# A fused attention and feed-forward block with its gradients: key weights in row pieces, five tiles only centred, two turned tiles copied by VectorE

## The chip, the cores and the metric

The kernel runs on one core of a Trainium2 chip. The metric is the device time of one execution in microseconds; lower is better. The core has five engines that run side by side, each with its own queue in order: TensorE (PE; its weight loads are PEld) multiplies matrices, VectorE (DVE) and ScalarE (ACT) work on tiles of 128 partitions, GpSimd (POOL) does small or slow elementwise work, and SyncE (SP) mostly issues transfers. Products land in PSUM; everything else lies in SBUF, 128 partitions wide. Sixteen DMA engines move data.

## The reference

x is 2048 rows of 640 features, bf16. The kernel returns the block's output and six gradients (the vector-Jacobian product with grad_out).

```python
def _A_ref(x, wqkv, wo):
    B, S, D = x.shape
    H = 32; Dh = D // H
    qkv = (x @ wqkv).reshape(B, S, 3, H, Dh).transpose(2, 0, 3, 1, 4)
    q, k, v = qkv[0], qkv[1], qkv[2]
    phi = lambda t: jnp.where(t > 0, t + 1, jnp.exp(t)) + 1e-6
    pq, pk = phi(q), phi(k)
    kv = jnp.einsum("bhsd,bhse->bhde", pk, v)
    z = jnp.einsum("bhsd->bhd", pk)
    num = jnp.einsum("bhqd,bhde->bhqe", pq, kv)
    den = jnp.einsum("bhqd,bhd->bhq", pq, z)[..., None] + 1e-6
    return (num / den).transpose(0, 2, 1, 3).reshape(B, S, D) @ wo
...
h = x + _A_ref(_layernorm(x), A_wqkv, A_wo)
h2 = h + _B_ref(_layernorm(h), B_w1, B_w3, B_w2)   # silu(x@w1) * (x@w3) @ w2
...
_out, _vjp = jax.vjp(_f, A_x, A_wqkv, A_wo, B_w1, B_w3, B_w2)
```

(The first lines are shortened: the reference writes the transposes through small lambdas.)

## The kernel before

The order of the work is written out by hand: each engine executes its instructions in the order in which the Python code emits them, and the framework adds the waits between engines. The rows of x form 16 tiles of 128 rows (ST = 16); the 640 features form 5 chunks of 128 (DT = 5) or two halves of 320 (HD).

The change lies in the first stage, which computes, for each tile t of x: the layernorm, the transposed normalized tile, the key product (tile times the 640 key columns of wqkv), and phi of it, stored in pk_all. Query tiles are interleaved from tile 6 on, at t = 6, 7, 9 and 11 (QT).

**Statistics and norm (class Stats).** Per tile VectorE runs two BatchNormStats over 320 columns each (L148), an aggregate (L151) and an addition of eps (L154, ve); POOL raises it to -0.5 (L155, rs). The norm (L161) subtracts the mean and multiplies by rs on VectorE, in place in x_sb. For even tiles from 10 on ScalarE does the norm instead (norm_act, L166), with a bias that POOL makes. Tile 0 is only centred (RAW = 1): its rs is applied as the scale of ScalarE's Exp and Relu instead, and p1_scale (L264, "C" in the steps) multiplies x by rs later on VectorE, since later work reads the scaled x.

**Turning a tile.** For tiles 0 to 7, p1_tr makes five transposes on TensorE into a PSUM tile (L258) and ScalarE copies them to pqT (L260). Tiles 8 to 15 are turned by a DMA transpose that SP issues after the norm (L251).

**Key product.** p1_mm makes two halves of five matmuls each (L268, 128x320), with the next tile's turning between them ("between"). The accumulators ("big") have two buffers. Tile 0 has its own path (first, kh, act): two separate PSUM tiles and four activations of 320 columns (L535).

**phi.** ScalarE computes Exp into mq and Relu into rq (L295, L296). The rest is held back: VectorE's min-and-add (L299) and the addition into pk_all or, for a query, into its own tile (L300). mq and rq have three buffers each, used in turn by all phis: those of key tiles 0 to 6, query 0, key 7, query 1, key 8 and so on.

**v_steps.** For each t this table lists what VectorE does after the key product was emitted: ("S", t) statistics of a tile, ("N", t) its norm, ("C", t) the scaling, R the oldest rest that is held. "A", "B" and "L" are norms placed behind the phi of that step.

**Beside it.** At t = 3 to 6 a chunk of another product (gp, L395, five matmuls of 512 columns) is computed and copied by ScalarE (L420). From t = 7 on m_part accumulates pk transposed times x (macc, L430) for the tiles in M0.

**Loads.** SP issues, in this order: x tiles 0 and 1, the key weights' first half of columns (load_wq(2, 3): all five row chunks, 320 columns), x tile 2, their second half, x tile 3, x tiles 4 and 5; then transposed loads of w2 and of grad_out, x tiles 6 to 9, the query weights (load_wq(0, 2)), x tiles 10 to 15. The weights w1 and w3 follow at t = 4, 5, 6 and 12 (trickle).

**The start.** TensorE runs 34 products of 128 columns on ones while the first loads come in (warm_up, L468), and 8 more after the turning of tile 0.

**The end.** The last stage makes 128-row jobs of the gradients of w1 and w3 (grad_job); the first seven jobs store their result in two halves each.

Of the kernel before, what the change touches and what calls it, by code (L numbers as in the profile page):

```python
# [9 lines left out]
P = 128  # L10
BF16 = mybir.dt.bfloat16
F32 = mybir.dt.float32
ALU = mybir.AluOpType
AF = mybir.ActivationFunctionType
# [4 lines left out]
S, D, H, F = 2048, 640, 32, 1728  # L19
DH = D // H  # L20
ST, DT = S // P, D // P
# [3 lines left out]
HD = D // 2  # L25
# [30 lines left out]
def kernel(  # L56
# [19 lines left out]
    V, A, T, G, SY = nc.vector, nc.scalar, nc.tensor, nc.gpsimd, nc.sync  # L76
    dma, dmaT, dmaG = SY.dma_start, SY.dma_start_transpose, G.dma_start
# [36 lines left out]
    x_sb = x_ext[:, :, 0:D]  # L114
# [16 lines left out]
    class Stats:  # L131
# [10 lines left out]
                for j in range(2):  # L142
                    self.part(src, t, j)

        def part(self, src, t, j, mid=None):
            if j == 0:
                self.st[t] = cp.tile([P, 2, 6], F32, name="st6", bufs=4)
            V.bn_stats(out=self.st[t][:, j, :], in_=src[:, t, j * HD:(j + 1) * HD])  # L148
            if j == 0:
                return  # L150
            V.bn_aggr(out=self.mv[:, t, :], in_=self.st.pop(t)[:])  # L151
            if mid is not None:
                mid()
            V.tensor_scalar(out=self.ve[:, t:t + 1], in0=self.mv[:, t, 1:2], scalar1=EPS_LN, scalar2=None, op0=ALU.add)  # L154
            G.tensor_tensor(out=self.rs[:, t:t + 1], in0=self.ve[:, t:t + 1], in1=mhalf[:, 0:1], op=ALU.pow)  # L155

        def center(self, out, src, t):
            V.tensor_scalar(out=out, in0=src, scalar1=self.mv[:, t, 0:1], scalar2=None, op0=ALU.subtract)
# [14 lines left out]
    ln1, ln2 = Stats("ln1"), Stats("ln2")  # L173
# [5 lines left out]
    ps = pool("p1p", space=PSUM)  # L179
    wqkv = U1.tile([P, DT, 3 * D], BF16, name="wqkv", tag="D")  # L180
    wq_v = A_wqkv.rearrange("(c p) n -> p c n", p=P)

    def load_wq(a, b):
        dma(out=wqkv[:, :, a * HD:b * HD], in_=wq_v[:, :, a * HD:b * HD])

    def load_x(a, b):
        dma(out=x_sb[:, a:b, :], in_=xS[:, a:b, :])

    load_x(1, 2)
    A.activation(sg[:], zero[:], AF.Exp)  # L190
    load_wq(2, 3)
    load_x(2, 3)
    load_wq(3, 4)
    load_x(3, 4)
    load_x(4, 6)

    mask = cp.tile([P, DT, M_MAX], BF16, name="mask")

# [40 lines left out]

    XT_DMA = 8  # L240
    WARM = 34
    RAW = 1

    def on_act(t):
        return t > XT_DMA and t % 2 == 0
# [1 line left out]
    def p1_norm(t):  # L247
        xn = x_sb[:, t, :]
        (ln1.norm_act if on_act(t) else ln1.norm)(xn, xn, t)
        if t >= XT_DMA:  # L250
            dmaT(out=pqT[:, :, t * P:(t + 1) * P], in_=xn)  # L251

    def p1_tr(t, parts=((0, DT),)):
        xn = x_sb[:, t, :]
        for a, b in parts:
            tr = ps.tile([P, DT, P], BF16, name="tr", bufs=2)
            for c in range(a, b):
                T.transpose(tr[:, c, :], xn[:, c * P:(c + 1) * P], ident[:])  # L258

            A.copy(out=pqT[:, a:b, t * P:(t + 1) * P], in_=tr[:, a:b, :])  # L260

    def p1_scale(t):
        xn = x_sb[:, t, :]
        V.tensor_scalar(out=xn, in0=xn, scalar1=ln1.rs[:, t:t + 1], scalar2=None, op0=ALU.mult)  # L264

    def p1_half(acc, t, n0):
        for c in range(DT):
            T.matmul(acc, lhsT=pqT[:, c, t * P:(t + 1) * P], rhs=wqkv[:, c, n0:n0 + HD], start=(c == 0),  # L268
                     stop=(c == DT - 1))

    def p1_acc():
        return ps.tile([P, 2, 512], F32, name="big", bufs=2)

    def p1_mm(t, n0, between=None, halves=None):
        acc = p1_acc() if halves is None else None
        for j in range(2):
            p1_half(acc[:, j, 0:HD] if halves is None else halves[j][:, 0:HD], t, n0 + j * HD)
            if j == 0 and between is not None:
                between()
        return acc  # L280

    def two(ap):
        return ap.rearrange("p (j n) -> p j n", j=2)
# [3 lines left out]
    def phi_tiles():  # L287
        return [p1.tile([P, D], BF16, name=n, bufs=3) for n in ("mq", "rq")]

    def phi(acc, dst, t, parts=None):  # L290

        mq, rq = parts or phi_tiles()
        if parts is None:
            kw = dict(scale=ln1.rs[:, t:t + 1]) if t < RAW else {}
            A.activation(two(mq[:]), acc[:, :, 0:HD], AF.Exp, **kw)  # L295
            A.activation(two(rq[:]), acc[:, :, 0:HD], AF.Relu, **kw)  # L296

        def rest():
            V.tensor_scalar(out=mq[:], in0=mq[:], scalar1=1.0, scalar2=1e-6, op0=ALU.min, op1=ALU.add)  # L299
            V.tensor_tensor(out=dst, in0=mq[:], in1=rq[:], op=ALU.add)  # L300
        held.append(rest)
# [157 lines left out]
    zero_pads()  # L459
    load_w2T(0, 2 * P)  # L460
    load_g2T(0)
    load_x(6, 10)
    load_w2T(2 * P, 4 * P)
    load_wq(0, 2)
    load_x(10, ST)
    def warm_up(n, warm):
        for _ in range(n):
            T.matmul(warm[:, 0:P], lhsT=ones[:], rhs=ones[:], start=True, stop=True, skip_group_check=True)  # L468
# [12 lines left out]
    def stat(t):  # L481
        ln1.run(x_sb, t, t + 1)
        if on_act(t):
            ln1.bias(t)
# [1 line left out]
    ln1.part(x_sb, 0, 0)  # L486
    ln1.part(x_sb, 0, 1, center_first)
    p1_tr(0, ((0, 2), (2, DT)))
    warm_up(8, p1_acc()[:, 0])
    stat(1)  # L490
    p1_norm(1)
    ln1.part(x_sb, 2, 0)
    ln1.part(x_sb, 2, 1)
    ln1.part(x_sb, 3, 0)
    p1_norm(2)
    ln1.part(x_sb, 3, 1)
    ln1.part(x_sb, 4, 0)
    p1_norm(3)
    ln1.part(x_sb, 4, 1)
    w13 = [go for c0, c1 in ((0, 2), (2, 4), (4, 5)) for go in load_w13(c0, c1)]  # L500
    w13 += [lambda: dma(out=w1[:, :, F:FP], in_=rows(B_w3)[:, :, F - FL:F])]

    def load_wo():
# [2 lines left out]
    trickle = {4: w13[0], 5: lambda: w13[1](0, 1), 6: lambda: w13[1](1, 2), 12: w13[2]}  # L506

    R = None
    v_steps = {1: (R, ("N", 4)), 2: (("S", 5), R, ("N", 5)), 3: (("S", 6), R, ("N", 6), ("C", 0)),
               4: (("S", 7), R, ("N", 7), ("S", 8)), 5: (R, ("N", 8), ("S", 9)), 6: (R, ("N", 9), ("S", 10)),  # L510
               7: (("S", 11), R, R, ("A", 10), ("L", 11)), 8: (("S", 12), R, R, ("S", 13)),
               9: (("N", 13), R, ("S", 14), ("B", 12)), 10: (R, R, ("S", 15)), 11: (R, ("A", 14), ("L", 15))}
    V_OPS = {"S": stat, "N": p1_norm, "C": p1_scale}

    def xn_out(g, q):
        sl = slice(g * TPC, (g + 1) * TPC)
# [9 lines left out]
    M0 = {7: (0, 1, 2), 8: (3, 4, 5)}  # L526
    M0.update({t: (t - 3,) for t in range(9, ST)})
    for t in range(ST):
        first = None
        if t < RAW:  # L530
            first = phi_tiles()
            kh = [ps.tile([P, 512], F32, name="k0", tag="m", bufs=2) for _ in range(2)]

            def act(i, j):
                A.activation(first[i][:, j * HD:(j + 1) * HD], kh[j][:, 0:HD], (AF.Exp, AF.Relu)[i],  # L535
                             scale=ln1.rs[:, t:t + 1])

            def between():
                act(0, 0)
                p1_tr(t + 1)  # L540
                act(1, 0)
            k = p1_mm(t, D, between, kh)
            act(0, 1)
            act(1, 1)
        else:
            k = p1_mm(t, D, (lambda: p1_tr(t + 1)) if t + 1 < XT_DMA else None)
        steps = v_steps.get(t, (R,) * len(held))
        for step in steps:
            if step is R:
                held.pop(0)()  # L550
            elif step[0] in V_OPS:
                V_OPS[step[0]](step[1])
        phi(k, pk_all[:, t, :], t, first)
        for when in ("A", "B", "L"):
            for step in steps:
                if step is not R and step[0] == when:
                    p1_norm(step[1])
            if when == "A" and t in QT:
                q_tile(QT.index(t))
        if 3 <= t < 7:  # L560
            ghh_chunk(t - 3, lambda: ps.tile([P, 512], F32, name="gp", tag="m", bufs=2))
        m_part(0, M0.get(t, ()))
        if t >= 11:
            V.memset(bd[:, t - 11, :], 0.0)
            make_mask(t - 11)
        if t >= 9:
            m_part(1, [2 * (t - 9), 2 * (t - 9) + 1])
        for f, *n in outs.get(t, ()):
            f(*n)
        if t in trickle:  # L570
            trickle[t]()
# [983 lines left out]
    for i, (f0, f1) in enumerate(blocks):  # L1555
        n = f1 - f0
        for m in range(DT):
            last = (i, m) == (len(blocks) - 1, DT - 1)
            for a, b in ((0, n - P), (n - P, n)) if last else ((0, n),):
                c = (a + b) // 2  # L1560
                halves = ((a, c), (c, b)) if i * DT + m < 7 else ((a, b),)
                out = [(x + y - a, z + y - a, to) for y, w in halves for x, z, to in both_grads(m, f0 + y, f0 + w)]
                grad_job(hnN, m, lambda t: gb[i][:, t, a:b], b - a, out, A.dma_start)
        load_block(i + 2)
        if 0 < i <= 4:
            gw2_out(i - 1)
        if i < 4:
            gw2_turn(i)
# [36 lines left out]
```

## Time and profile before

| what | value |
|---|---|
| median of 3 runs | 820.98 us (819.28 to 821.57) |
| the profiled execution | 820.36 us |
| its span | 818.64 us |
| PE busy | 811.6 us (99%) |
| DVE busy | 452.7 us (55%) |
| ACT busy | 324.8 us (40%) |
| POOL busy | 131.7 us (16%) |
| granted TensorE clock | 1.00 |

The span is the time from the first to the last instruction in the profile; the execution's own time has 1.7 us more around it. Times in the profile are counted from the start of the span. An engine's busy time says little by itself: what counts is which engine or transfer the chain of work goes through at a given moment. In lines of the timeline the first number is the start, the second the time of one instruction or of a group of equal ones; overlapping neighbours on one engine start before the previous one's recorded end.

### The profile page before, as it was taken

Reading aid. Unit: us, or ns where it says so; the run is one execution under the profiler, and the core shown is the slowest. Engines: PE = TensorE matmul, PEld = TensorE weight load, DVE = VectorE, ACT = ScalarE, POOL = GpSimd, SP = SyncE. Lnnn points to the kernel's source line nnn. Section 1 sums busy time; section 2 is a strip of 40 time slices with the busy share of each in tenths; the row PEclk is TensorE's granted clock in tenths of the full one; section 3 lists DMA queues with packets and bytes.
Section 4 is the critical chain, followed back from the end, with each engine's and each line's share of the span. In section 5 each row is a group of like instructions: output and inputs, shape, how many; then the busy total and the mean of one; then the engine's idle time right before and its main releaser. Section 6 shows DMA issues by size and latency. Waiting matters only on the chain.

```text
span 818.6 us, 13711 instructions
## 1 busy us (share of the span) xinstructions
PE 811.6 (99%) x5261; PEld 501.6 (61%) x5292; DVE 452.7 (55%) x973; ACT 324.8 (40%) x609; POOL 131.7 (16%) x198
## 2 busy tenths in 40 slices
PE   9999999999999999999999999999999999999998
PEld 6777544555555555754577777777777777544444
DVE  7859997998898566300057777772781544200000
ACT  7856688665565666011112212222212334211111
POOL 2243333323222212100001111110220000000000
PEclk9999999999999999999999999999999999999999
DMA  9899899696485556999877877269994888979991
GB/s 262 207 242 277 206 276 302 207 244 174 128 209 158 169 168 168 239 254 243 233 178 181 218 194 193 58 111 181 269 217 93 179 193 153 249 175 235 221 239 37
DMA packets 335889, 162.46 MB, mean 198 GB/s; under 512 B 252560, under 2 KB 329072, under 8 KB 335824
## 3 DMA queue, kind: packets, MB, share of 16 engines
q1 hardware_dynamic: 291920, 120.68, 63.8%
q0 software_dynamic: 7328, 24.48, 8.9%
q10 hardware_dynamic: 36576, 16.42, 8.2%
q8 instruction: 41, 0.67, 0.3%
q14 instruction: 24, 0.20, 0.1%
HBM read 47.09 MB, written 53.43 MB: 123 GB/s over the span
## 4 chain that ended last, share of the span: by engine, by line
PE 96%; DMA 1%; ACT 1%; DVE 1%; issue 0%; SPq 0%; POOL 0%; DVEq 0%
PE mm L395 20%; PE job L1335 19%; PE ghn L1131 14%; PE gxn L1504 8%; PE gw L1086 7%; PE big L268 4%; PE o L913 4%; PE o L859 3%; PE gwo L1219 3%; PE macc L430 3%; PE gr L1188 3%; PE dkv L1441 3%; PE at L657 2%; DMA wqkv<-in_A_wqkv_dram 1%; PE dkv L1369 1%; DMA tri<-tri 1%
## 5 line engine op out<-in xcount | busy, mean ns | idle before, releaser
L1335 PE MATMUL job<-gb,hnN 128*128 128x496 bf16 (+3 forms) x576 | 116.8, 366 | 0.0
L1131 PEld LDWEIGHTS <-ggb 128*128 128x128 bf16 x864 | 84.5, 98 | 33.0
L395 PE MATMUL mm<-pqT,w 128*128 128x512 bf16 x396 | 93.2, 379 | 0.5
L1335 PEld LDWEIGHTS <-hnN 128*128 128x128 bf16 x576 | 55.8, 98 | 61.0
L395 PEld LDWEIGHTS <-w 128*128 128x128 bf16 x540 | 52.6, 98 | 62.9 <-issue 0.6
L1339 ACT CAST obs<-job 128x496 bf16<-128x496 f32 (+4 forms) x56 | 28.5, 510 | 123.6 <-PE job L1335 123.6
L1131 PE MATMUL ghn<-w13a,ggb 128*128 128x320 bf16 x448 | 63.5, 299 | 0.0
L1146 DVE SCALAR_TENSOR_TENSOR wb<-gs,hnb 128x640 f32<-128x640 bf16 x16 | 13.2, 825 | 88.1 <-ACT gs L1143 88.1
L1131 PE MATMUL ghn<-w13b,ggb 128*128 128x320 bf16 x416 | 61.4, 299 | 0.0
L395 PE MATMUL mm<-g2T,w2T 128*128 128x512 bf16 x228 | 58.8, 379 | 0.6
L1086 PE MATMUL gw<-hb,g 128*128 128x512 bf16 (+2 forms) x316 | 58.4, 345 | 0.2
L1086 PEld LDWEIGHTS <-g 128*128 128x128 bf16 x320 | 31.3, 98 | 27.0
L420 ACT CAST ghh<-mm 128x512 bf16<-128x512 f32 x48 | 28.2, 588 | 48.2 <-PE mm L395 41.4
L1196 POOL TENSOR_TENSOR sz<-Zb,g_h 128x640 f32<-128x640 bf16 x16 | 20.2, 1262 | 163.7 <-DVE g_h L1197 163.7
L796 ACT ACTIVATE sig<-mm 128x512 bf16<-128x512 f32 x56 | 33.7, 602 | 25.0 <-PE mm L395 21.6
L1143 ACT ACTIVATE gs<-ghn 128x640 bf16<-128x640 f32 x16 | 11.3, 705 | 76.0 <-PE ghn L1131 76.0
L395 PEld LDWEIGHTS <-w2T 128*128 128x128 bf16 x260 | 25.4, 98 | 23.4
L268 PEld LDWEIGHTS <-pqT 128*128 128x128 bf16 x320 | 30.7, 98 | 13.5 <-ACT pqT L260 0.9
L268 PE MATMUL big<-wqkv,pqT 128*128 128x320 bf16 x250 | 38.4, 299 | 0.2
L1335 PEld LDWEIGHTS <-g 128*128 128x128 bf16 x320 | 31.0, 98 | 11.5
L832 DVE TENSOR_TENSOR gate<-gate,sig 128x1024 bf16<-128x1024 bf16 x28 | 19.3, 689 | 33.9 <-ACT gate L807 31.1
L1091 ACT CAST gw2o<-gw 128x512 bf16<-128x512 f32 (+2 forms) x20 | 10.4, 519 | 66.6 <-PE gw L1086 25.3
(217 smaller groups left out, 1391.2 us busy)
## 6 DMA issues: line engine op xcount, KB each, us to landing
hh_d<-hhT SPq DMA_DIRECT2D x24, 256.0 KB, 2.8
gg_d<-gate POOLq DMA_DIRECT2D x24, 256.0 KB, 4.4
gg_d<-ghh POOLq DMA_DIRECT2D x24, 256.0 KB, 4.1
ggb<-gg_d SPq DMA_DIRECT2D x6, 896.0 KB, 5.3
ggb<-gg_d ACTq DMA_DIRECT2D x6, 832.0 KB, 5.7
ggb<-gg_d SPq DMA_DIRECT2D x2, 1728.0 KB, 13.9
pk_d<-pk_all SPq DMA_DIRECT2D x4, 640.0 KB, 5.4
g<-in_grad_out_dram SPq DMA_DIRECT2D x4, 640.0 KB, 5.7
```

Of the source, the lines that this page charges most:

```text
L268: T.matmul(acc, lhsT=pqT[:, c, t * P:(t + 1) * P], rhs=wqkv[:, c, n0:n0 + HD], start=(c == 0), stop=(c == DT - 1))
L395: T.matmul(acc[:], lhsT=w[:, c, fc * P:(fc + 1) * P], rhs=rhs[:, c, :], start=(c == 0), stop=(c == DT - 1))
L420: A.copy(out=ghh[n // 2][:, n % 2, :], in_=acc[:])
L430: T.matmul(macc[m][j][:, 0:n], lhsT=pk_all[:, t, m * P:(m + 1) * P], rhs=x_ext[:, t, j * HD:j * HD + n], start=(t == 0), stop=(t == ST - 1))
L796: A.activation(sig[:, i, :], gp[:], AF.Sigmoid)
L859: T.matmul(accs[i, j][:, 0:HD], lhsT=hhT[c][:, fc, i * P:(i + 1) * P], rhs=w2[:, fc, j * HD:(j + 1) * HD], start=(first and fc == 0), stop ...
L913: T.matmul(o2["ps"][:, 0:HD], lhsT=hhT[c][:, fc, i * P:(i + 1) * P], rhs=w2[:, fc, j * HD:(j + 1) * HD], start=(fc == 0), stop=(fc == FT - 1))
L1086: T.matmul(acc[:, 0:fw], lhsT=g2[:, t, m * P:(m + 1) * P], rhs=hb[b][:, t, 0:fw], start=(t == 0), stop=(t == ST - 1))
L1131: T.matmul(acc[:, j, 0:HD], lhsT=ggb[t // 2][:, k, lo:lo + P], rhs=rhs[:, j * HD:(j + 1) * HD], start=(k == 0), stop=(k == NG - 1))
L1335: T.matmul(acc[:, 0:n], lhsT=lhs[:, t, m * P:(m + 1) * P], rhs=rhs(t), start=(t == 0), stop=(t == ST - 1))
L1339: A.copy(out=ob, in_=acc[:, 0:n])
L1504: T.matmul(acc[:, j, 0:HD], lhsT=g, rhs=wqT[:, k, j * HD:(j + 1) * HD], start=(k == 0), stop=(k == 14))
```

## The change

- The key weights come in two row pieces: row chunks 0 and 1 with all 640 columns ahead of x tile 2, chunks 2 to 4 behind it. The x loads are regrouped (4 to 6, then 7 to 9), and the query weights come in two loads.
- Tile 0's product goes chunk by chunk over both halves (first_mm), with the turning of tile 1 behind the first two chunks; its special phi path goes.
- Tiles 0 to 4 are only centred (RAW = 5); their rs goes into Exp and Relu, and POOL instead of VectorE scales x for these five tiles, at t = 3 to 6.
- The turned tiles 2 and 3 are copied by VectorE; the others still by ScalarE.
- From t = 3 on, the turning of the next tile comes behind both halves of the key product instead of between them.
- Statistics, norms and rests stand one step later in v_steps for t up to 7, with the query rests following.
- Four warm-up products instead of eight behind the turning of tile 0.
- In the last stage six instead of seven jobs store in two halves.

```diff
-        def part(self, src, t, j, mid=None):
+        def part(self, src, t, j, mid=None, end=True):
...
-            if j == 0:
-                return
+            if j and end:
+                self.end(t, mid)
+
+        def end(self, t, mid=None):
             V.bn_aggr(out=self.mv[:, t, :], in_=self.st.pop(t)[:])
             if mid is not None:
                 mid()
...
+    def load_wk(a, b):
+        dma(out=wqkv[:, a:b, D:2 * D], in_=wq_v[:, a:b, D:2 * D])
+
     load_x(1, 2)
     A.activation(sg[:], zero[:], AF.Exp)
-    load_wq(2, 3)
+    load_wk(0, 2)
     load_x(2, 3)
-    load_wq(3, 4)
+    load_wk(2, DT)
     load_x(3, 4)
-    load_x(4, 6)
+    load_x(4, 7)
...
-    RAW = 1
+    RAW = 5
...
-    def p1_tr(t, parts=((0, DT),)):
+    def p1_tr(t, parts=((0, DT),), copy=A.copy):
...
-            A.copy(out=pqT[:, a:b, t * P:(t + 1) * P], in_=tr[:, a:b, :])
+            copy(out=pqT[:, a:b, t * P:(t + 1) * P], in_=tr[:, a:b, :])
...
-        V.tensor_scalar(out=xn, in0=xn, scalar1=ln1.rs[:, t:t + 1], scalar2=None, op0=ALU.mult)
+        G.tensor_scalar(out=xn, in0=xn, scalar1=ln1.rs[:, t:t + 1], scalar2=None, op0=ALU.mult)
...
-    def p1_mm(t, n0, between=None, halves=None):
-        acc = p1_acc() if halves is None else None
+    def p1_mm(t, n0, between=None, at=0):
+        acc = p1_acc()
         for j in range(2):
...
-            if j == 0 and between is not None:
+            if j == at and between is not None:
                 between()
         return acc
 
+    def first_mm(between):
+        acc = p1_acc()
+        for c in range(DT):
+            for j in range(2):
+                T.matmul(acc[:, j, 0:HD], lhsT=pqT[:, c, 0:P], rhs=wqkv[:, c, D + j * HD:D + (j + 1) * HD],
+                         start=(c == 0), stop=(c == DT - 1))
+            if c == 1:
+                between()
+        return acc
...
-    load_x(6, 10)
+    load_x(7, 10)
     load_w2T(2 * P, 4 * P)
-    load_wq(0, 2)
+    load_wq(0, 1)
+    load_wq(1, 2)
...
-    warm_up(8, p1_acc()[:, 0])
-    stat(1)
-    p1_norm(1)
-    ln1.part(x_sb, 2, 0)
-    ln1.part(x_sb, 2, 1)
-    ln1.part(x_sb, 3, 0)
-    p1_norm(2)
-    ln1.part(x_sb, 3, 1)
-    ln1.part(x_sb, 4, 0)
-    p1_norm(3)
-    ln1.part(x_sb, 4, 1)
+    warm_up(4, p1_acc()[:, 0])
+    for t in (1, 2):
+        ln1.part(x_sb, t, 0)
+        ln1.part(x_sb, t, 1, lambda: center(t))
+    ln1.part(x_sb, 3, 0)
+    ln1.part(x_sb, 3, 1, end=False)
...
-    v_steps = {1: (R, ("N", 4)), 2: (("S", 5), R, ("N", 5)), 3: (("S", 6), R, ("N", 6), ("C", 0)),
-               4: (("S", 7), R, ("N", 7), ("S", 8)), 5: (R, ("N", 8), ("S", 9)), 6: (R, ("N", 9), ("S", 10)),
-               7: (("S", 11), R, R, ("A", 10), ("L", 11)), 8: (("S", 12), R, R, ("S", 13)),
-               9: (("N", 13), R, ("S", 14), ("B", 12)), 10: (R, R, ("S", 15)), 11: (R, ("A", 14), ("L", 15))}
-    V_OPS = {"S": stat, "N": p1_norm, "C": p1_scale}
+    v_steps = {1: (("E", 3), ("P", 4, 0)), 2: (("P", 4, 1), ("E", 4), R), 3: (("S", 5), R, ("N", 5), ("C", 0)),
+               4: (("S", 6), R, ("N", 6), ("C", 1)), 5: (("S", 7), R, ("N", 7), ("S", 8), ("C", 2), ("C", 3)),
+               6: (R, ("N", 8), ("S", 9), ("C", 4)), 7: (R, R, ("N", 9), ("S", 10), ("S", 11), ("A", 10), ("L", 11)),
+               8: (("S", 12), R, R, ("S", 13)), 9: (("N", 13), R, ("S", 14), ("B", 12)), 10: (R, R, ("S", 15)),
+               11: (R, R, ("A", 14), ("L", 15))}
+    V_OPS = {"S": stat, "N": p1_norm, "C": p1_scale, "E": lambda t: ln1.end(t, lambda: center(t)),
+             "P": lambda t, j: ln1.part(x_sb, t, j, end=False)}
...
+        turn = (lambda: p1_tr(t + 1, copy=V.tensor_copy if t in (1, 2) else A.copy)) if t + 1 < XT_DMA else None
+        k = p1_mm(t, D, turn, int(t > 2)) if t else first_mm(turn)
...
-                halves = ((a, c), (c, b)) if i * DT + m < 7 else ((a, b),)
+                halves = ((a, c), (c, b)) if i * DT + m < 6 else ((a, b),)
```

## The prediction

> **What bounds the kernel now.** I read the page's chain first, then busy time by window, the chain in order of time up to 16 us, the timelines of VectorE and ScalarE from 27 to 33 us, and who ScalarE waits for.
>
> ```profile
> PE 96%; DMA 1%; ACT 1%; DVE 1%; issue 0%; SPq 0%; POOL 0%; DVEq 0%
> 0.00:15.00 15.00, 12.99 (x109) 9.81 (x111) 10.44 (x39) 10.33 (x18) 3.77 (x12) 1.00 0.93 233
> 15.00:42.00 27.00, 26.95 (x197) 18.64 (x197) 24.38 (x77) 23.14 (x37) 6.98 (x14) 1.00 0.86 229
> ```
> The first line is the chain by engine; the others give window, length and then busy us of PE, PEld, DVE, ACT, POOL. TensorE carries the chain, so whatever idles it moves the end. From 15 to 42 us it idles 0.05 us; VectorE is busy 24.38 of 27, so it has little room in just the stage to which the change gives it other work.
>
> ```profile
> 2.77 5.33 DMA wqkv<-in_A_wqkv_dram
> 8.10 0.04 issue
> 8.14 0.84 PE k L268 x5
> ...
> 9.99 0.69 ACT pqT L260
> 10.68 0.69 ACT mq L295
> 11.38 0.59 ACT rq L296
> 11.97 0.67 ACT pqT L260
> 12.63 0.05 issue
> 12.68 0.85 PE big L268 x5
> ```
> The head's chain (start, us): the second half of the key weights lands at 8.10, and from 9.99 to 12.63 ScalarE is what TensorE waits for: two copies of turned tiles with an Exp and a Relu between them. That is what the change attacks.
>
> ```profile
> 28.14 0.32 DVE L299 TENSOR_SCALAR mq<-mq 128x640 bf16<-128x640 bf16 x1
> 28.56 0.49 DVE L300 TENSOR_TENSOR pk_all<-mq,rq 128x640 bf16<-128x640 bf16 x1
> 28.97 0.32 DVE L299 TENSOR_SCALAR mq<-mq 128x640 bf16<-128x640 bf16 x1
> 29.40 0.49 DVE L300 TENSOR_TENSOR hx<-mq,rq 128x640 bf16<-128x640 bf16 x1
> 29.81 0.44 DVE L161 TENSOR_SCALAR x_sb<-x_sb,ln_mv,ln_rs 128x640 bf16<-128x640 bf16 x1
> 30.16 0.88 DVE L148 BATCH_NORM_STATS2 st<-x_sb 128x6 f32<-128x320 bf16 x2
> ```
> VectorE's timeline: the rest of phi (min, add) of key tile 6, of query tile 0 (it writes hx), then the norm of tile 11 and the statistics of tile 12.
>
> ```profile
> ACT mq L295 <- DVE pk_all L300: 2.4, 4, 0.8
> ```
> ScalarE's waits from 24 to 44 us (total, times, longest). mq and rq have three buffers each, so an Exp waits for the rest three phis before it. Key tile 8's Exp is the eleventh phi, query tile 0's the eighth: Exp 8 (30.34 in ScalarE's timeline) needs the rest that ends at 29.89. The ring has almost no slack now.
>
> **How I cost it.** I list each engine's instructions in their new order; each starts when its engine is free and its inputs are there (+0.04 us, the chain's "issue" steps). Start-to-start times come from the timeline: half product 0.68, turning a tile 0.28, gp 1.08, macc 0.82; ScalarE Exp or Relu 0.60 (0.69 with a scale), copy 0.68; VectorE statistics pair 0.92, aggregate 0.24, eps 0.08, min 0.42, add 0.41, norm 0.36; POOL's rs 0.56. The same list for the old order gives norm 9 at 25.32 (trace 25.34), Exp 8 at 30.31 (30.34), the products of tile 9 at 30.64 (30.74): good to about 0.2 us.
>
> **The change, part by part.**
>
> *Row pieces.* Both pieces move the same 800 KB, in packets of 1280 B instead of 640 B. The packet records give 55 and 32 ns, so an engine needs 40 x 55 = 2.20 us instead of 80 x 32 = 2.56. I take the second piece at 8.10 - 0.36 = 7.75 (bounds 7.0, if the long first packets of the slowest engine go away, and 8.1), the first, two rows of five, at 6.2 instead of 6.58. The third x tile that shares a load with tiles 4 and 5 adds 0.44 us there, and tile 4 is first read at 10.9; splitting the query weights adds an issue of 0.58 us on SP and 0.36 us of packets, before a use at 22.
>
> *Only centred, copies on VectorE.* Tile 1 no longer waits for its rs. Scaling moves into Exp and Relu (0.79 against 0.70 us each, on a ScalarE that has lost two copies). VectorE's copy out of PSUM has no row at 128x640; L1422 takes 0.280 us for 256 columns and 0.345 for 384, which continues to 0.48 (bounds 0.35 and ScalarE's 0.69). TensorE then runs: rest of tile 0 at 7.79, tile 1 at 8.61, turn of tile 2 at 9.29 to 9.57, VectorE's copy 9.78 to 10.26, tile 2 at 10.33, copy of tile 3 11.50 to 11.98, tile 3 at 12.02: **0.6 us earlier** than in the list of before (12.64). But the first copy is queued in front of the aggregate and centring of tile 3, so VectorE idles 0.6 us until tile 2 is turned.
>
> *Transposes behind the products.* From tile 4 on, gp (1.08 us) hides ScalarE's copy (0.69). Tile 5's turning wants, at 16.10, a norm that VectorE ends at 16.39: 0.3 us lost. What is left is **0.3 us earlier** from tile 5 to tile 8.
>
> *The rests one step later.* v_steps takes the first rest at tile 2 instead of 1, so at tile 7 the two rests are those of tiles 5 and 6, not 6 and query 0. VectorE starts norm 9 at 26.49 instead of 25.32: 0.83 for the rest of tile 6 that now stands ahead of it, 0.34 for the two copies (0.82) less the scaling that went (0.30) and an earlier start. Then the rest of query 0 comes behind norm 11 (0.36) and the statistics of tile 12 (1.24), and norm 11 follows eps 11 directly, so that VectorE stands 0.75 us waiting for rs 11 (POOL 0.56 and both hops). It ends at 29.90 + 0.34 + 0.36 + 1.24 + 0.75 = **32.59**. Behind it on ScalarE waits Exp 8: 32.63 to Relu's end at 33.93, 2.3 us late; and Exp of query 1 waits behind ScalarE's norm of tile 10 (rs 10 late), until a Relu end of 31.23. TensorE has two accumulators: tile 9 is ready at 30.31 and starts at 31.27 (0.96), query 2 at 32.63 and starts at 33.97 (1.34), query 3 at 39.69 and starts at 40.27 (0.58). 2.88 - 0.33 = **2.55 us later**, by tile 12.
>
> *Scaling on POOL.* Five tensor_scalar of 128x640. Rows around it: a memset of 64x512 0.54 us, a two-input product of 128x640 1.26; I take 0.9. Three (tiles 0, 1, 2) run beside statistics. But tiles 2 and 3 follow each other, and rs 9 and tile 4 stand behind them.
> ```profile
> 59.94 1.86 DVE L299 TENSOR_SCALAR mq<-mq 128x640 bf16<-128x640 bf16 x1
> 60.07 1.54 POOL L367 TENSOR_TENSOR pr<-hx,Zb 128x320 f32<-128x320 bf16 x2
> ```
> Here the min, 0.32 us elsewhere, took 1.86 while POOL multiplied: it waited for both products. With that, the rest of tile 5 waits 0.65 us for tile 3's scaling and the add of tile 6 waits 0.8 for tile 4's: +1.45, so 4.0 us later in all. Bounds: 0 (the form doesn't collide, or VectorE comes first) and +2.75 (at 1.26 us each). The row is the nearest, but who comes first is open; I take +0.9.
> The Trainium skill (GPSIMD Engine Reference, 3.1 Elementwise) puts a GpSimd loop with little work at 1.03 cycles an element, at 1.2 GHz an estimate of 0.55 us for 640; by it the sum would be 3.0 us instead of 4.0. No row here shows the form.
>
> *Hidden.* Tile 8's DMA transpose is issued at 23.7 (before 23.39) behind one more weight load; at 2.6 us to landing, or 3.8 behind that load, it is there by 27.5, wanted at 28.1. POOL's scalings end by 27.5; tiles 0 to 2 are read at 27.3 with their own done at 24.6. Storing the seventh weight-gradient job in one piece lies in 640 to 815 us, where TensorE is busy all 175 us and ScalarE 43.75: nothing. Without that cover, one issue is about half a microsecond.
>
> **Sum.** -0.33 + 2.88 + 0.9 = +3.4 us, of which nothing is won back: after 42 us TensorE idles 5 us in all, in waits behind its own work. The profiled execution took 820.36 us (span 818.64 and 1.7 around it): 823.8. The median of the runs lies 0.62 above it, 824.4. I say **824.1**. Of before, 0.3% is 2.46 us, about what a measurement of this kernel can tell from no change.
>
> **Rivals.**
> *It bites less* (0.22). No collision on POOL, and early weights: 7.0 also moves VectorE's first waits, and the list gives +1.8 to +2.55 for 7.0 to 7.75, 822.2 to 823.4. For it: POOL's small rs never lengthened a neighbour. Against: the two L299 lines.
> *Head gain alone* (0.12). Exp 8 finds its buffer free: this decides at about 30.3 us, when the rest of query 0 must be done. Then 0.3 to 1.1 us are won, 819.9 to 820.7, and with much earlier weights 818.5. For it: ScalarE's stretch 9.99 to 12.63 does go. Against: VectorE would have to be 2.3 us ahead of the list.
> *POOL scaling is dear* (0.06). At 2.0 us each, rs 9 and the rests queue up behind it: list +9, 829. For it: POOL's pace on products, 2 ns an element; against: one input, not two.
> *Late clock* (0.04). Matmuls of 128 columns are 107 ns apart until 6.1 us and 56 from 7.3 on: the faster pace came 5.1 us after the first product (1.13). Four of the eight warm-up products go, which leaves TensorE idle just before 6.2. If it had to start afresh there, all up to 11.3 would run at half pace; the 3.5 us from 7.79 on would do 1.75 us of work: 825.8. Against: the gap is 0.3 us. The Trainium skill (TensorE: Matmul & The Clock Gate, Part 1) has the pace set by free-running windows of 3.4 us; by it the delay would end at 9.6, an estimate of 0.9 us. No run here shows either.
>
> **Numbers.** Forecast 0.56 (own range 823.4 to 826). Slower by over 0.3%: 0.56 + 0.06 + 0.04 = 0.66. Within: 0.22 and 0.08 of the head gain, 0.30. Faster: the remaining 0.04. The range leaves out the better half of the head gain and dear scaling: 820.4 to 826.8.
>
> **What would show it.** Right: tile 3's products near 12.0; a VectorE wait for rs 11; min of query 0 after 31.5; an Exp of ScalarE waiting over 1 us for VectorE's add; TensorE idle some 3 us between 30 and 41. POOL's scaling: its duration, and a min or add above 0.5 us beside it. Wrong: TensorE without gaps there, or gaps before 28 us (then norms 5 to 7 are later than listed).

## The result and the profile after

The changed kernel takes 826.01 us (median of 5 runs, 825.74 to 826.90). The kernel before, run beside it, takes 820.44 us (819.26 to 821.57). The ratio is 1.0074, 95% interval 1.0062 to 1.0085: 0.74% slower. The profiled execution took 826.61 us, its span is 824.5 us, against 818.64 before: 5.86 us more.

Line numbers from here on are those of the changed kernel unless said otherwise: L148 statistics, L153 aggregate, L156 eps, L157 rs on POOL, L160 centring, L163 norm, L168 the norm that ScalarE does, L265 the copy of a turned tile, L269 the scaling on POOL, L273 and L291 the products, L309 and L310 Exp and Relu, L313 and L314 min and add of a rest, L444 the gradient products (macc).

The page's chain of work by engine:

```profile
PE 93%; DVE 3%; DMA 2%; ACT 1%; issue 0%; SPq 0%; POOL 0%; DVEq 0%; ACTq 0%
```

Busy time by window (length, then PE, PEld, DVE, ACT, POOL, the granted clock, DMA share and GB/s):

```profile
0.00:15.00 15.00, 12.73 (x106) 9.95 (x108) 10.04 (x37) 8.69 (x14) 3.48 (x11) 1.00 0.91 228
15.00:42.00 27.00, 22.62 (x160) 14.82 (x160) 23.83 (x68) 18.98 (x31) 16.39 (x18) 1.00 0.74 200
```

VectorE's share of the chain went from 1% to 3%. From 15 to 42 us TensorE is busy 22.62 us where it was 26.95, and POOL 16.39 instead of 6.98. VectorE works nearly as long as before in this window (23.83 against 24.38), but gets less far.

The chain in order of time in the head (start, us):

```profile
2.71 5.47 DMA wqkv<-in_A_wqkv_dram
8.19 0.04 issue
8.23 0.98 PE big L291 x6
9.20 0.68 PE big L273 x5
9.88 0.28 PE tr L263 x5
10.16 1.51 PE big L273 x10
11.67 0.29 PE tr L263 x5
11.96 0.02 issue
11.99 0.49 DVE pqT L265
12.48 0.41 DVE st L148
```

The second piece of the key weights is there at 8.19, not earlier than before (8.10). ScalarE's copies have left the head of the chain, as meant, but at 11.99 VectorE enters it and carries it up to 39.6 us, apart from 17.4 to 24.2, where it runs through TensorE and one copy on ScalarE, and two rs on POOL. What that does to TensorE is in its timeline; the last brackets are idle time and who ended it:

```profile
29.44 1.52 PE L273 MATMUL big<-wqkv,pqT 128*128 128x320 bf16 x10
30.80 0.98 PE L444 MATMUL macc<-x_sb,pk_all 128*128 128x320 bf16 x6
34.54 1.52 PE L273 MATMUL big<-wqkv,pqT 128*128 128x320 bf16 x10 [2.76 <-ACT rq L310]
37.00 1.52 PE L273 MATMUL big<-wqkv,pqT 128*128 128x320 bf16 x10 [0.94 <-ACT rq L310]
```

These are tile 8, the gradient products, tile 9 and query 2. With 0.33 us at query 3 the stalls are 4.03 us. Tile 12 starts at 45.37 where it started at 39.98 (the first line is of the kernel before): **5.4 us of the 5.86 are lost by then**.

```profile
39.98 1.52 PE L268 MATMUL big<-wqkv,pqT 128*128 128x320 bf16 x10
45.37 1.52 PE L273 MATMUL big<-wqkv,pqT 128*128 128x320 bf16 x10
```

ScalarE's waits from 24 to 44 us (total, times, longest) say whom it waited for:

```profile
ACT x_sb L168 <- POOL nb L172: 2.8, 1, 2.8
ACT mq L309 <- DVE hx L314: 2.7, 2, 1.5
```

The 2.8 us are the norm of tile 10, which ScalarE does itself: it stands in front of query 1's Exp and waits for a bias that POOL can only make after VectorE's statistics of tile 10. The 2.7 us are Exp 8 (1.16) and query 2's Exp (1.54), which wait for adds. VectorE's own timeline shows why all of it is late:

```profile
24.62 0.92 DVE L163 TENSOR_SCALAR x_sb<-x_sb,ln_mv,ln_rs 128x640 bf16<-128x640 bf16 x1
...
26.68 0.72 DVE L313 TENSOR_SCALAR mq<-mq 128x640 bf16<-128x640 bf16 x1
27.51 0.49 DVE L314 TENSOR_TENSOR pk_all<-mq,rq 128x640 bf16<-128x640 bf16 x1
27.92 0.58 DVE L313 TENSOR_SCALAR mq<-mq 128x640 bf16<-128x640 bf16 x1
28.60 0.49 DVE L314 TENSOR_TENSOR pk_all<-mq,rq 128x640 bf16<-128x640 bf16 x1
29.01 0.92 DVE L163 TENSOR_SCALAR x_sb<-x_sb,ln_mv,ln_rs 128x640 bf16<-128x640 bf16 x1
```

Norm 9 begins at 29.01. In the kernel before it was this line:

```profile
25.34 0.44 DVE L161 TENSOR_SCALAR x_sb<-x_sb,ln_mv,ln_rs 128x640 bf16<-128x640 bf16 x1
```

Norms that took 0.44 us take 0.92, mins that took 0.32 take 0.72 and 0.58, while the adds are 0.49 as ever. Beside them POOL scales:

```profile
16.30 1.96 POOL L269 TENSOR_SCALAR x_sb<-x_sb,ln_rs 128x640 bf16<-128x640 bf16 x1
...
24.50 3.81 POOL L269 TENSOR_SCALAR x_sb<-x_sb,ln_rs 128x640 bf16<-128x640 bf16 x2
28.29 0.62 POOL L157 TENSOR_TENSOR ln_rs<-ln_ve,mhalf 128x1 f32<-128x1 f32 x1
28.91 1.94 POOL L269 TENSOR_SCALAR x_sb<-x_sb,ln_rs 128x640 bf16<-128x640 bf16 x1
```

One scaling takes 1.9 us. Against their times in the kernel before, four norms are longer by 0.48 and two mins by 0.40 and 0.26: 2.58 us that VectorE loses.

### The profile page after: what moved, and what is told of

Its sections match the earlier page's. It is cut to its first block, busy times and chain, and to the rows that moved or that the text cites. A ratio compares the mean times of both kernels' runs of the same rounds, so it can differ in the third digit from the quotient of the medians.

```text
span 824.5 us, 13717 instructions
## 1 busy us (share of the span) xinstructions
PE 812.3 (99%) x5257; PEld 501.1 (61%) x5288; DVE 455.7 (55%) x974; ACT 323.8 (39%) x605; POOL 141.0 (17%) x203
## 4 chain that ended last, share of the span: by engine, by line
PE 93%; DVE 3%; DMA 2%; ACT 1%; issue 0%; SPq 0%; POOL 0%; DVEq 0%; ACTq 0%
PE mm L409 20%; PE job L1331 19%; PE ghn L1127 14%; PE gxn L1500 8%; PE gw L1082 7%; PE o L909 4%; PE o L855 3%; PE gwo L1215 3%; PE gr L1184 3%; PE dkv L1437 3%; PE big L273 2%; PE macc L444 2%; PE at L653 2%; DVE st L148 1%; DMA wqkv<-in_A_wqkv_dram 1%; PE mm L273 1%
## 5 line engine op out<-in xcount | busy, mean ns | idle before, releaser
L273 PE MATMUL big<-wqkv,pqT 128*128 128x320 bf16 x250 | 38.1, 299 | 4.0 <-ACT rq L310 4.0
L273 PEld LDWEIGHTS <-pqT 128*128 128x128 bf16 x310 | 29.9, 98 | 17.0 <-issue 3.9
## 6 DMA issues: line engine op xcount, KB each, us to landing
ggb<-gg_d ACTq DMA_DIRECT2D x6, 832.0 KB, 5.7
```

## The experiments

All are read by two numbers: the median of the runs, and the start of tile 12's products in the one profiled execution, which shows what the first 45 us cost without the scatter of what follows. It does contain the scatter of the first loads: VectorE's first copy of a turned tile waits for them, and in the profiles that have this copy it starts between 9.10 and 10.20 us (10.20 in the change). "Later" is against 39.98 in the kernel before. The median of the kernel before was 820.44 beside the changed kernel, 820.28 beside the first four runs, 820.05 beside the next four, 819.88 beside the last four.

| kernel | median us (range, runs) | ratio to before (95%) | tile 12 at | later |
|---|---|---|---|---|
| the change | 826.01 (825.74–826.90, 5) | 1.0074 (1.0062–1.0085) | 45.37 | 5.39 |
| no_scale | 824.22 (823.17–826.01, 5) | 1.0050 (1.0038–1.0062) | 42.71 | 2.73 |
| scale_vec | 825.46 (824.25–827.43, 5) | 1.0069 (1.0056–1.0082) | 44.17 | 4.19 |
| rest_early | 826.87 (824.03–828.76, 6) | 1.0076 (1.0060–1.0092) | 44.71 | 4.73 |
| copy_act | 825.17 (823.57–825.94, 5) | 1.0062 (1.0049–1.0075) | 43.86 | 3.88 |
| cols | 827.00 (825.40–827.57, 4) | 1.0081 (1.0066–1.0096) | 44.90 | 4.92 |
| rows_only | 822.60 (821.03–824.71, 9) | 1.0028 (1.0014–1.0042) | 40.42 | 0.44 |
| norm10_behind | 825.75 (825.29–828.40, 5) | 1.0076 (1.0059–1.0093) | 45.69 | 5.71 |
| keep_busy | 829.92 (829.24–832.01, 4) | 1.0124 (1.0108–1.0140) | 44.96 | 4.98 |
| turn_mid | 825.25 (824.90–827.46, 5) | 1.0069 (1.0056–1.0081) | 44.92 | 4.94 |
| light2 | 822.33 (821.78–824.38, 5) | 1.0036 (1.0022–1.0049) | 41.04 | 1.06 |
| light3 | 822.18 (821.95–824.64, 6) | 1.0032 (1.0020–1.0043) | 40.77 | 0.79 |
| pool_scale_alone | 825.05 (823.98–826.03, 5) | 1.0062 (1.0048–1.0076) | 44.52 | 4.54 |

**no_scale: the scalings left out.**

```diff
-    V_OPS = {"S": stat, "N": p1_norm, "C": p1_scale, "E": lambda t: ln1.end(t, lambda: center(t)),
+    V_OPS = {"S": stat, "N": p1_norm, "C": lambda t: None, "E": lambda t: ln1.end(t, lambda: center(t)),
```

> The five scalings of tiles 0 to 4 are left out (x of these tiles stays centred only, in what the gradient products and the stored copy of x read). Theory V (VectorE's own sum of work before norm 9 sets how late everything after it is; the scalings on POOL stretch what VectorE runs beside them): norms 5, 6, 8 and 9 go back from 0.92 to 0.44 us and the two long mins from 0.72 and 0.58 to 0.32, norm 9 starts near 26.9 instead of 29.01, time 823.0 to 824.0. Rival O (the rests put one step later are the cause, the scalings only lie beside): norm 9 moves by under 0.7, tile 9 still waits over 2 us, time 825.2 to 826.0.

Tile 12 came 2.66 us earlier, the median 1.8. VectorE's norms in this run:

```profile
23.61 0.44 DVE L163 TENSOR_SCALAR x_sb<-x_sb,ln_mv,ln_rs 128x640 bf16<-128x640 bf16 x1
...
26.85 0.44 DVE L163 TENSOR_SCALAR x_sb<-x_sb,ln_mv,ln_rs 128x640 bf16<-128x640 bf16 x1
```

The second is norm 9: 26.85, 2.16 us earlier than in the change, where 2.10 of the 2.58 us of stretch lie ahead of it (the norms of tiles 5, 6 and 8 and the two mins). So the stretch is the scalings', and VectorE's lateness passes to tile 12 nearly one to one. The median lies 0.2 above theory V's range.

**scale_vec: the scalings on VectorE.**

```diff
-        G.tensor_scalar(out=xn, in0=xn, scalar1=ln1.rs[:, t:t + 1], scalar2=None, op0=ALU.mult)
+        V.tensor_scalar(out=xn, in0=xn, scalar1=ln1.rs[:, t:t + 1], scalar2=None, op0=ALU.mult)
```

> The five scalings go to VectorE, at the same places of its order. Theory V: 2.6 us of stretch less, 5 times 0.38 us of scaling more (before's row of the one scaling that VectorE did), so 0.7 us less in all, time 824.8 to 825.8, a little below the changed kernel. Rival P (POOL's 1.9 us each are late for their readers, the gradient products, whatever VectorE does): time 823 to 824.

825.46, as theory V had it. All norms are back at 0.44, and the scalings take 0.38 us each on VectorE; tile 12 comes 1.2 us earlier, 0.17 of it from an earlier first copy. The totals alone don't tell this run from the change, since their intervals overlap. Five scalings at 0.38 cost VectorE less than POOL's five cost it by lying beside its norms. POOL's duration for its own readers is not what counts here.

**rest_early: the rests as before from step 7 on.**

```diff
-               6: (R, ("N", 8), ("S", 9), ("C", 4)), 7: (R, R, ("N", 9), ("S", 10), ("S", 11), ("A", 10), ("L", 11)),
+               6: (R, ("N", 8), ("S", 9), ("C", 4)), 7: (R, R, R, ("N", 9), ("S", 10), ("S", 11), ("A", 10), ("L", 11)),
...
-               11: (R, R, ("A", 14), ("L", 15))}
+               11: (R, ("A", 14), ("L", 15))}
```

> Three rests instead of two in step 7, so that from there on the rests run as in the kernel before. Rival O (the prediction's reading: query 0's rest behind norm 11 and the statistics of tile 12 is what Exp 8 and tile 9 wait for): Exp 8 no longer waits, tile 9's wait falls from 2.76 to under 1, time 823.5 to 824.6. Theory V (statistics 10 come late from a full VectorE, and ScalarE's norm 10 stands ahead of query 1's Exp): norm 10 starts 0.8 us later still, tile 9 waits 3.5, the waits of query 2 and 3 shrink by about 1 each, time 824.8 to 826.2.

No gain: the interval covers the change's. The profiled execution (824.72) is one of the two fastest of six, and VectorE's first copy starts 1.10 us earlier in it than in the change, but tile 12 only 0.66. ScalarE's timeline in this run:

```profile
31.79 0.92 ACT L168 ACTIVATE x_sb<-x_sb,nb,ln_rs 128x640 bf16<-128x640 bf16 x1 [3.49 <-POOL nb L172]
32.62 0.77 ACT L309 ACTIVATE mq<-big,ln_rs 128x640 bf16<-128x640 f32 x1
33.29 0.78 ACT L310 ACTIVATE rq<-big,ln_rs 128x640 bf16<-128x640 f32 x1
33.97 0.70 ACT L309 ACTIVATE mq<-big 128x640 bf16<-128x640 f32 x1
```

Exp 8 (the last line) waits no longer, as theory O wanted. But the rest of query 0 now stands ahead of the statistics of tile 10, so that norm 10 waits 3.49 us instead of 2.81, and TensorE 3.19 ahead of tile 9. The wait moved; its sum is VectorE's. This run also shows something else, by window (columns as above, the granted clock third from the right):

```profile
28.00:31.00 3.00, 2.94 (x22) 1.87 (x20) 2.83 (x8) 0.30 (x1) 2.26 (x2) 1.00 0.28 98
31.00:34.00 3.00, 0.00 (x0) 0.10 (x1) 2.23 (x8) 2.21 (x4) 1.20 (x3) 0.92 0.19 43
34.00:37.00 3.00, 2.88 (x12) 1.66 (x12) 2.72 (x9) 1.27 (x4) 1.02 (x2) 0.52 0.73 171
```

After the idle stretch the clock is at one half from 33.49 to 36.90 us. The 20 products of tile 9 and query 2 take 4.22 us there instead of 2.88.

**copy_act: ScalarE copies tiles 2 and 3.**

```diff
-        turn = (lambda: p1_tr(t + 1, copy=V.tensor_copy if t in (1, 2) else A.copy)) if t + 1 < XT_DMA else None
+        turn = (lambda: p1_tr(t + 1, copy=A.copy)) if t + 1 < XT_DMA else None
```

> The turned tiles 2 and 3 are copied by ScalarE, all else as changed. Theory V: VectorE gets 2 times 0.49 us and about 0.7 us of waiting for the turns back, norm 9 starts 1.0 to 1.7 earlier, time 824.3 to 825.2. Rival H (tile 2 and 3 are turned later from ScalarE, whose Exp and Relu stand ahead; TensorE loses 0.3 to 0.6 per tile in the head): time 826.0 to 826.8.

Theory V: tile 12 came 1.5 us earlier, norm 9 1.49 (27.52), the median 0.8. TensorE does lose time in the head (0.58 and 0.15 us of waiting for ScalarE's copies), and it makes no difference, because VectorE sets the pace after it.

**cols: column pieces again.**

```diff
-    load_wk(0, 2)
+    load_wq(2, 3)
     load_x(2, 3)
-    load_wk(2, DT)
+    load_wq(3, 4)
...
-        k = p1_mm(t, D, turn, int(t > 2)) if t else first_mm(turn)
+        k = p1_mm(t, D, turn, int(t > 2))
```

> The changed kernel with the key weights in two column pieces again (each 320 columns of all five chunks), tile 0 multiplied half by half; all else as changed. Theory V (VectorE's queue sets the pace from 12 to 42 us): TensorE's head may be up to 0.5 us later or earlier, the end moves by under 0.5, 825.6 to 826.5. Rival L (the loads of the head, second weight piece at 8.2 and x tile 3 behind it, are where the time was lost): 823.5 to 825.

827.0 (interval 1.0066 to 1.0096): not better, so the row pieces are not what costs 5.6 us. Tile 12 is 0.47 us earlier, and so is VectorE's first copy (9.72 against 10.20). The median is 0.5 above theory V's range; in the profiled run 2.1 us of waits for two transposing transfers between 80 and 95 us come on top (see rows_only).

**rows_only: the loads and tile 0's product alone.** The kernel before with the new loads, first_mm and four warm-up products; its norms, copies, steps and its one scaling on VectorE stay.

```diff
-    load_wq(2, 3)
+    load_wk(0, 2)
     load_x(2, 3)
-    load_wq(3, 4)
+    load_wk(2, DT)
...
-    load_x(4, 6)
+    load_x(4, 7)
...
+        k = p1_mm(t, D, turn) if t else first_mm(turn)
```

> The kernel before with the row pieces, the loads regrouped as in the change, tile 0 multiplied by chunks and its Exp and Relu whole, 4 warming products instead of 8; norms, ScalarE's copies, transposes between the halves, the order of VectorE's steps and the one scaling on VectorE stay as before. Theory V: no stall at tiles 8 to 12, the end within 0.5 us of the kernel before, 819.9 to 820.8. Rival L (loads): later by a part of the 5.6, 821.5 to 824.

Neither theory as it stood. Tile 12 is 0.44 us later, and nothing stalls at tiles 8 to 12, as theory V had it. But the median is 2.5 us up (0.28%, interval 0.14 to 0.42), which is rival L's size, though not in its place. The rest of it arises at 80 to 92 us, where TensorE waits 1.54 and 0.33 us for the transposed Wp. These lines give the time that Wp's transfers took to land, from 70 to 100 us, first in the kernel before:

```profile
DMA to landing us min/median/max: 2.6/3.1/4.5
```

The same view of this run, with TensorE's idle time until Wp came (us, times):

```profile
  DMA Wp<-pkx: 1.9, 2
...
DMA to landing us min/median/max: 2.7/4.9/5.4
```

In the profiles that show this wait (the change, no_scale, scale_vec, cols, rows_only, keep_busy, light2, light3) the first transfer of Wp is issued 0.7 to 1.9 us behind a 960 KB reload of x and the median landing is 4.0 to 5.0 us. In those that don't (before, copy_act, rest_early, norm10_behind, turn_mid, pool_scale_alone) it is 1.9 to 2.3 us and 2.8 to 3.3. The two groups touch: 1.90 us in the change, with the wait, and 1.88 in norm10_behind, without. A collision with the reload, which depends on when this stage is reached, fits these numbers but was not shown: no run moved the reload. How much of the change's 5.6 us in the total is due to the loads stays open, and totals tell the kernels apart only to a microsecond or two.

**norm10_behind: ScalarE's norm 10 behind query 1.**

```diff
-("S", 11), ("A", 10), ("L", 11)),
+("S", 11), ("B", 10), ("L", 11)),
```

> Norm 10 goes behind query 1's Exp and Relu in ScalarE's order, nothing else. Rival N (the place: ScalarE's norm 10, waiting 2.8 us for its bias, holds back query 1's Exp and with it tile 9): tile 9 starts near 31.8 instead of 34.5, time 823.5 to 824.5. Theory V: tile 9 is earlier too, but query 2, tile 10 and query 3 wait for VectorE's adds instead, and the stalls' sum stays near 4: time 825.2 to 826.2.

Tile 9 starts at 31.76 as rival N expected, 2.8 us earlier. Then query 2 starts only at 36.34, after 3.04 us of waiting; in the change it started at 37.00. The total is theory V's, 825.75. The clock fell here too, and query 2's ten products take 2.83 us instead of 1.52, so that tile 12 comes no earlier than in the change; but the two runs at a mean clock of 1.0 take 825.29 and 825.74. Counted from VectorE's first copy (9.54 here), query 2 starts after 26.80 us in both kernels. Taking out the one largest wait gains nothing, because the engine behind it is the same.

**keep_busy: products of ones in the stall.**

```diff
+        if t == 9:
+            warm_up(30, ps.tile([P, 512], F32, name="warm", tag="tr", bufs=2))
         k = p1_mm(t, D, turn, int(t > 2)) if t else first_mm(turn)
```

> 30 products of ones by ones (128 columns each, 1.7 us, read by nobody) stand ahead of tile 9's, in the stall. Theory C (an idle stretch of about 3 us lets the granted clock fall to one half for some 3.4 us, as in the run with three rests, where 1.4 us were lost by it; most runs of the changed kernel have a mean clock of 0.998): every run at mean clock 1.0, time 824.6 to 825.5. Rival (VectorE is behind anyway, so a slower TensorE costs nothing): 825.8 to 826.4.

Neither. Tile 12 starts 0.4 us before the change's, as VectorE's first copy does (9.81 against 10.20), so the 30 products cost nothing where they stand. But the runs take 829.2 to 832.0, and one of the four still has a mean clock of 0.998. Between 80 and 98 us TensorE waits 3.2 us for mT (0.52) and Wp (1.20 and 1.52), where the change waits 1.0; Wp's first transfer is issued 0.7 us behind the x reload here, closer than in any other run. Why it comes so close was not settled, so this run says nothing on the clock.

**turn_mid: transposes between the halves again.**

```diff
-        k = p1_mm(t, D, turn, int(t > 2)) if t else first_mm(turn)
+        k = p1_mm(t, D, turn) if t else first_mm(turn)
```

> The turning of tiles 4 to 7 goes back between the two halves of the product before, all else as changed. The prediction had 0.3 us for this move (the later start of tile 5 to 8). Theory V: those 0.3 are hidden by VectorE's lateness, tile 12 starts where it did in the changed kernel (45.4) within 0.5, time 825.5 to 826.5. If the 0.3 count: 825.4 to 825.8, tile 12 at 45.0; the two differ by little and only the trace can tell them apart.

Tile 12 at 44.92, 825.25, a little under both ranges. The 0.45 us at tile 12 are within what the head scatters: VectorE's first copy starts 0.74 us earlier than in the change (9.46), and counted from it query 2 starts after 26.79 us here and 26.80 in the change. So the 0.3 us are hidden, as theory V had it. Here, too, the clock fell (tile 9 and query 2):

```profile
33.80 2.22 PE L273 MATMUL big<-wqkv,pqT 128*128 128x320 bf16 x10 [2.27 <-ACT rq L310]
36.25 2.30 PE L273 MATMUL big<-wqkv,pqT 128*128 128x320 bf16 x10 [0.23 <-ACT rq L310]
```

Stalls of 2.27 and 0.23 us and 1.48 us of half speed (2.22 and 2.30 against 1.52) make 3.98; the change's profile has 4.03 us of stalls at full clock. The slow products took the place of waiting: another sign that TensorE isn't what sets the pace.

**light2 and light3: scalings out and copies on ScalarE; then the third rest too.** The edits of no_scale and copy_act together, then with that of rest_early.

> Both loads of VectorE are taken away at once: the five scalings left out (x of tiles 0 to 4 only centred in what the gradient products and the stored copy read) and the two copies on ScalarE. Theory V (their costs at tile 12 add up: 5.4 less 2.65 less 1.5): tile 12 starts 1.0 to 1.6 later than in the kernel before, that is at 41.0 to 41.6; time 821.5 to 823. Rival O (the rests one step later are a cause of their own size): tile 12 stays at least 2.2 later, time 823 to 824.

> As the run before, with the three rests in step 7 too. Theory V: with VectorE light again the rest of query 0 no longer waits behind norm 11, tile 12 at 40.4 to 41.0, 0.4 to 0.8 earlier than without the third rest; time 820.8 to 822.3. Rival O: the third rest brings 1.5 or more here, tile 12 at 40.0 or before.

light2 is theory V's: tile 12 at 41.04, 822.33. The two edits gave 2.66 and 1.51 alone and 4.33 together, so the costs add, as far as single profiles tell: VectorE waited 1.02 us for an x tile at 8 us in copy_act and not in light2. light3 brings tile 12 to 40.77, inside theory V's bounds, but the gain of 0.27 us is less than its 0.4, and the median stays.

**pool_scale_alone: the scalings alone, on the kernel before.**

```diff
-        V.tensor_scalar(out=xn, in0=xn, scalar1=ln1.rs[:, t:t + 1], scalar2=None, op0=ALU.mult)
+        G.tensor_scalar(out=xn, in0=xn, scalar1=ln1.rs[:, t:t + 1], scalar2=None, op0=ALU.mult)
...
-               4: (("S", 7), R, ("N", 7), ("S", 8)), 5: (R, ("N", 8), ("S", 9)), 6: (R, ("N", 9), ("S", 10)),
+               4: (("S", 7), R, ("N", 7), ("S", 8), ("C", 1)), 5: (R, ("N", 8), ("S", 9), ("C", 2), ("C", 3)),
+               6: (R, ("N", 9), ("S", 10), ("C", 4)),
```

> The kernel before with the scalings alone: POOL scales tiles 0 to 4 at steps 3 to 6 (tile 0 there instead of on VectorE; tiles 1 to 4, which are normed already, are multiplied by their factor once more, so the values of what reads them change). Theory V: each scaling takes 1.9 us, norms beside it 0.92 instead of 0.44, VectorE reaches norm 11 about 2 us later than 29.8; the kernel before has some slack there, so tile 12 starts 0.5 to 2 later than 39.98, time 820.5 to 822.5. Rival (the scalings hurt only because VectorE is late already): norm 11 late, tile 12 within 0.3, time 819.8 to 820.5.

Dearer than both: 825.05, tile 12 at 44.52. TensorE's timeline (lines of the kernel before: L430 gradient products, L268 products, L264 scaling):

```profile
29.92 0.44 PE L430 MATMUL macc<-x_sb,pk_all 128*128 128x320 bf16 x2
33.06 1.07 PE L430 MATMUL macc<-x_sb,pk_all 128*128 128x320 bf16 x4 [2.71 <-POOL x_sb L264]
33.93 4.23 PE L268 MATMUL big<-wqkv,pqT 128*128 128x320 bf16 x20
```

Here everything else is on time, so the gradient products of tile 4 come to wait for POOL itself: its scaling ends at 33.0, behind two others and an rs. VectorE waits 2.24 us for rs 11, which stands behind the same scaling. Then the clock falls, and the next 20 products take 4.23 us instead of 2.88; all five runs have a mean clock of 0.998. In the change that wait is not seen: its scaling of tile 4 ends at 30.85, as the gradient products start (30.80). One part of the change, put alone on the kernel before, costs nearly as much as the whole.

## Why the prediction was right, and where it was not

The direction, the place and the chain held: VectorE runs late, ScalarE's Exp waits for it, TensorE idles. The time is 826.0 against a forecast of 824.1: inside the whole range, at the upper end of the forecast's own (823.4 to 826), and 5.6 us of loss where 3.4 were added up. Most of the signs named in advance are there: VectorE waits 0.67 us for rs 11, the min of query 0 starts at 34.64 (after 31.5), Exp 8 waits 1.16 and query 2's Exp 1.54 us for adds, TensorE idles 4.03 us between 30 and 44, and POOL's scaling has mins beside it of 0.72 and 0.58. One sign is missing: tile 3's products start at 12.54, not near 12.0. And one that was named for being wrong is there: TensorE has a gap before 28 us, 0.61 at 17.39, because norm 5 ends at 17.34 and not at the 16.39 of the list, which had 0.3 us of this gap.

*Row pieces.* "I take the second piece at 7.75": it landed at 8.19 in the profiled run, outside the bounds (7.0 to 8.1). In other profiles with row pieces the products that need it start between 7.12 and 8.59, so the landing scatters more than the gain that was worked out. It mattered through VectorE, whose first copy waits until the tile behind these products is turned. In five profiles (the change, cols, norm10_behind, keep_busy, turn_mid) this copy starts between 9.46 and 10.20 us, and query 2's products always 26.79 to 26.81 us behind it. So the 0.44 us that the landing was late are in the stall. The list had that slope: 1.8 us of lateness for 7.0, 2.55 for 7.75.

*Copies on VectorE.* 0.48 us was worked out, 0.49 measured, and VectorE's idling for the turns was seen (0.69 and 0.30). But tile 3 started 0.14 us earlier than before (12.54 against 12.68), not 0.6, and the price was mis-placed: the text put 0.34 us of VectorE's lateness on copies and scaling together, while taking the copies back gave 1.5 to 1.7 us at tile 12.

*Transposes behind the products.* The wait for norm 5 is there and is 0.61 us instead of 0.3, since norm 5 starts late and takes 0.92 us. Tile 8 starts 0.88 us later than before (29.44 against 28.56), where the text had 0.3 earlier.

*The rests one step later.* The list said 2.55 us for all but the scaling, and no_scale measured 2.73, with the weights' products at 8.18, for which the list's slope makes an estimate of 2.98: the sum was close. Its reading was not. The text made the rest of query 0 behind norm 11 the cause; the third rest gains 0.27 us on a light VectorE and nothing on a full one. The 2.73 are the copies (1.67, no_scale to light2), the loads and first_mm (0.44, rows_only), the third rest (0.27) and 0.35 that no run separates; as differences of single profiles these are rough.

*Scaling on POOL: the step that was mis-sized.* "I take 0.9" us for one; it takes 1.94, more than the upper bound of 1.26 and about the 2.0 of the rival "POOL scaling is dear". And "+0.9" for its effect was 2.66. The way was another, too: the prediction had VectorE stand still until POOL is done, which for 2.0 us each gave +9. In the change's profile only norms and mins lengthen, by 0.26 to 0.48 us, while adds and statistics don't. With the duration too short and the collision too hard the two errors partly cancelled, and that the time still came out inside the range is in part luck. The Trainium skill (GPSIMD Engine Reference, 3.1 Elementwise), by which one scaling would have been an estimate of 0.55 us, does not agree with the trace, which has 1.88 to 1.96, always with VectorE at work beside it; no run shows the scaling alone.

*Sum.* -0.33 + 2.88 + 0.9 was the forecast; 2.73 + 2.66 was found at tile 12, and 0.5 more behind it, net of what is won back, with 0.78 us of waits for Wp in the profile. The one store fewer in the last stage was not tried alone; what it does lies in this remainder.

*Late clock.* This rival had the right kind of event in the wrong place. In the change's profile the clock is full from 6.43 us to the end of the work. In rest_early, norm10_behind, turn_mid and pool_scale_alone it fell in or behind the stall, for 3.41 us. Four of the change's five runs have a mean clock of 0.998, which fits one such fall; where it lies in them is not on record. It hardly shows in the totals: the one run at 1.0 is among the slower of the five.

No variant beat the kernel before; the nearest, rows_only, is 0.28% slower.

## What to carry to other kernels

When the engine behind the bound has little slack in a stage (here 2.6 of 27 us), count what a change puts on that engine, not which wait it removes: a wait taken away came back one step later here (rest_early, norm10_behind) until the work itself went (light2). Moving work to an idle engine is not free if it lengthens its neighbours' instructions; measure the moved form beside the neighbours first. And one profile of an early stage, compared at a fixed landmark and counted from where the engine that sets the pace is held up first, tells more than totals that a later collision scatters by a microsecond or two.

## What the hardware showed beyond expectation

- POOL's multiplication of 128x640 bf16 by one number per partition takes 1.88 to 1.96 us beside VectorE's work (2.19 and 2.27 once each); VectorE does the same in 0.38. A norm on VectorE that starts 0.1 us behind such a scaling takes 0.92 instead of 0.44 us, and a min inside it 0.58 to 0.72 instead of 0.32; in the change's profile the add of two tiles (0.49) and the statistics (0.44 each) keep their time. It isn't always so: inside the scaling of 2.27 us in rest_early a min (0.32) and a norm (0.43) keep theirs, and the add between them takes 0.82. What decides it was not found.
- The granted clock moves in a fixed grid. In rest_early, turn_mid and pool_scale_alone the trace's clock record has full clock for 27.307 us, then one half for 3.413: eight such windows to one. In norm10_behind the full stretch is 30.720, nine of them. Laid on this grid, the window before the fall had TensorE idle for 2.27 (turn_mid), 2.56 (rest_early), 2.66 (norm10_behind) and 2.71 us (pool_scale_alone). In the change's profile the stall of 2.76 us falls across two windows, with 1.95 us of idleness in the first, and full clock was kept. So where a stall falls in the grid counts, not its length alone. The Trainium skill (TensorE: Matmul & The Clock Gate, Part 1) describes such free-running windows of about 3.4 us, and here the trace agrees.
